# Hash attention and a gated block on Trainium2: the sign bits of two key chunks and two heads as four products on 32 rows each, side by side

## The chip, the cores and the metric

The kernel runs on one core of a Trainium2 chip. The core has TensorE (PE, matrix products), VectorE (DVE, elementwise work), ScalarE (ACT, activation functions and copies), GpSimd (POOL) and SyncE (SP). In this kernel POOL and SP mostly issue transfers (DMAs); ACT issues four at the start. Matmuls accumulate into PSUM, which has eight banks on each of its 128 partitions (rows); all else is held in SBUF, also of 128 partitions. The metric is the time of one execution on the device in microseconds. Each engine works through its own list of instructions in order, and waits on semaphores for what others have to deliver.

## The reference

There are 4 batches, 8 heads, 768 positions and a head width of 64. Each query and each key is projected on 6 directions, and the 6 signs make up its bucket. A query attends only to keys of its own bucket:

```
q_bits = einsum(q, proj) > 0            # 6 bits a query
k_bits = einsum(k, proj) > 0            # 6 bits a key
mask   = bucket(q_bits) == bucket(k_bits)
scores = where(mask, q @ k.T / sqrt(64), -1e9)
attn   = exp(scores - max) / sum
x      = (attn @ v), heads side by side # 3072 x 512
out    = (silu(x @ w_gate) * (x @ w_val)) @ w_out
```

The last line is the gated block, with 3072 tokens, 512 columns and 1536 hidden columns. The weights come in as doubles and are turned into fp32 parts on the chip, so that the products of the gated block can be made of several faster ones.

## The kernel before, in words

**Attention** goes through 16 pairs of heads (`pairs`: batch b, pair pr), two heads to a pair. The two heads of 64 dimensions lie above each other on the partitions: head 0 on rows 0 to 63, head 1 on rows 64 to 127, in the transposed tiles `qT` and `kT` (fp32, 128 x 768). A **unit** (`units`, line 503) is one pair n, one half of the queries (384) and one chunk c of 128 keys: 2 x 6 = 12 units a pair, 192 in all. Units 2i and 2i + 1 share pair and half, and their chunks are an even and the following odd one.

**A unit's scores** (`score`, line 533) are made in two steps. `products` (524) takes a two-bank PSUM buffer and puts into it keys times queries in fp32, head 0 into the one bank and head 1 into the other (`product`, 515, line 521). Each of these matmuls uses the 64 rows of its head, so that the two of them lie on different rows of the array. `mark` (528) then accumulates onto the same banks a bf16 product of sign bits: `kb` (bits of keys, times a large constant) with `qb` (bits of queries). It reaches its maximum only where all the signs agree, so after the exponential (L530, ACT) the weights of other buckets vanish. The exponential writes the weights `A` into a ring of 12 units.

**The bits.** One matmul with `hash_w` (`hash_blocks`, 427, L430) gives both heads' projections at once on a strip of 32 rows: rows 0 to 15 belong to head 0 and rows 16 to 31 to head 1. ACT takes the sign (L435) and puts it into rows 0 to 31 of `qb` or `kb` (`low`). The product of head h, however, reads rows h*64 to h*64 + 63, so the 32 rows must also stand at rows 64 to 95 (`high`). For queries a DMA on POOL's queue copies them (`spread_q`, L447). For keys two DVE instructions (`spread_k`, L444) write rows 64 to 95 and then rows 0 to 31, each multiplied with a column that keeps one head's 16 rows and zeroes the other's, and that brings in the large constant (`times_k`). The rest of the rows, 32 to 63 and 96 to 127, hold zeros from the start of the kernel, so that 64 rows can be multiplied. There are two tiles of each kind (`sides`), used in turn by even and odd pairs.

**Order.** The order is written out by hand (`manual_schedule`). For pair n the loop at line 632 transposes the raw tiles of pair n + 1 (`prepare_pair(2)`, DVE, L458), makes the 12 units' scores, adding up the weights on DVE between them (`add`, L563 to L570), then the sums over keys of pair n - 1 (`total`, L581), the projections of pair n + 1 (`hash_next` by way of `prepare_pair(1)`, L430) with the signs, and the spreads of the bits of pair n + 1. After that come pieces of weight preparation on ACT (`begin_pieces`) and DVE (`advance_pieces`), with their stores and loads on POOL's queue (L170, L130), and the twelve `attend` steps of pair n, which multiply the weights with the values (L545; here the two heads lie on 64 columns each). Pair 0 has a start of its own (`start_first`): its bits are spread by halves, and units 0 to 2 are made there.

**PSUM** is one pool of four buffers of two banks, taken in rotation: each unit's scores, the joint tile for sums and projections, the av tile, and later the tiles of the gated block.

**The gated block** follows when all pairs are done. It works on blocks of 1024 tokens, with matmuls on 128 rows and 128 columns (L690), and has no part in the change.

Of the kernel before, what the change touches and what calls it, by code (L numbers as in the profile page):

```python
# [13 lines left out]
ALU = mybir.AluOpType  # L14
# [5 lines left out]
def kernel(  # L20
# [20 lines left out]
    nc = tc.nc  # L41
    PSUM = bass.MemoryType.PSUM
    B, H, S, D = q.shape
    NBITS = proj.shape[1]
    P = 128
    NCH = S // P
    CH = NCH // 2
    HQ = CH * P
    BLOCK = 32
# [31 lines left out]
    def two_banks(name):  # L81
        return pp.tile([P, 2, 512], FP32, tag="pp", name=name)
# [21 lines left out]
    n = 0  # L104
# [197 lines left out]
    def attention(scope):  # L302
# [85 lines left out]
        mask, times_k = columns[2:4], columns[4:6]  # L388
# [3 lines left out]
        for h in range(2):  # L392
            rows = slice(h * D, (h + 1) * D)
# [18 lines left out]
        bits = {}  # L412
# [3 lines left out]
        def joint(n):  # L416

            if n not in joints:
                joints[n] = two_banks("joint")
            return joints[n]  # L420

        def front(n):
            bits["q", n] = sides["q", n % 2]
            bits["k", n] = sides["k", n % 2]
            low, high = slice(0, BLOCK), slice(D, D + BLOCK)

            def hash_blocks(todo):
                tile_ = joint(n - 2)[:, 1]
                for i, (name, half) in enumerate(todo):
                    nc.tensor.matmul(tile_[i * BLOCK : (i + 1) * BLOCK, 0:HQ], hash_w,  # L430
                                     T[name, n][:, half * HQ : (half + 1) * HQ],
                                     start=True, stop=True)

                def sign(i, name, half, to=low, **how):
                    nc.scalar.activation(bits[name, n][to, half * HQ : (half + 1) * HQ],  # L435
                                         tile_[i * BLOCK : (i + 1) * BLOCK, 0:HQ], AF.Sign,
                                         **(how or {"bias": nudge[name]}))

                return [lambda i=i, at=at, **how: sign(i, *at, **how) for i, at in enumerate(todo)]

            def spread_k(times, cols=slice(0, S)):
                b = bits["k", n][:, cols]
                for to, by in ((high, times[1]), (low, times[0])):
                    nc.vector.tensor_scalar(b[to], b[low], scalar1=by, scalar2=None, op0=ALU.mult)  # L444

            def spread_q():
                nc.gpsimd.dma_start(bits["q", n][high], bits["q", n][low])  # L447

            def hash_next(todo):
                q0, q1, *ks = hash_blocks(todo)  # L450
                q0()
                q1()
                spread_q()
                return ks + [lambda: spread_k(times_k)]

            def transpose_blocks(name):
                T[name, n] = opnd.tile([P, S], FP32, tag=name + "T", name=name + "T")
                nc.vector.transpose(T[name, n], raws[name, n].rearrange("p c h d -> p (c h d)"))  # L458

            def start_first():  # L460
                for half in range(2):
                    cols = slice(half * HQ, (half + 1) * HQ)
                    for name in "kq":
                        if not half:
                            T[name, n] = opnd.tile([P, S], FP32, tag=name + "T", name=name + "T")
                        ps = two_banks("tps")[:, 0]
                        for i in range(CH):
                            nc.tensor.transpose(ps[:, i * P : (i + 1) * P],
                                                raws[name, n][:, half * CH + i].rearrange("p h d -> p (h d)"),
                                                ident)  # L470
                        if name == "k":
                            nc.scalar.activation(T[name, n][:, cols], ps[:, 0:HQ], AF.Copy,
                                                 scale=2 / OFF)
                        else:
                            nc.vector.tensor_copy(T[name, n][:, cols], ps[:, 0:HQ])

                def both_heads(sign, name, half):
                    cols = slice(half * HQ, (half + 1) * HQ)
                    sign()
                    if name == "k":  # L480
                        spread_k(mask, cols)
                    else:
                        nc.vector.tensor_copy(bits["q", n][high, cols], bits["q", n][low, cols])

                products(0)
                todo = [("k", 0), ("q", 0), ("k", 1), ("q", 1)]
                signs = hash_blocks(todo)
                for i in range(2):
                    both_heads(signs[i], *todo[i])
                products(1)  # L490
                products(2)
                for i in range(3):
                    mark(i)
                    if i < 2:
                        both_heads(signs[2 + i], *todo[2 + i])

            order = [("q", 0), ("q", 1), ("k", 0), ("k", 1)]
            if n:
                return [lambda name=name: transpose_blocks(name) for name in "kq"] + [
                    lambda: hash_next(order)]  # L500
            return start_first()

        units = [(n, half, c) for n in range(len(pairs)) for half in range(2) for c in range(NCH)]
# [6 lines left out]
        def weights(u):  # L510
            return ring[u % RING]

        banks_of = {}

        def product(u, x, start):
            n, half, c = units[u]
            qs = slice(half * HQ, (half + 1) * HQ)
            ks = slice(c * P, (c + 1) * P)
            for h in range(2):
                rows = slice(h * D, (h + 1) * D)  # L520
                nc.tensor.matmul(banks_of[u][:, h], x["k", n][rows, ks], x["q", n][rows, qs],  # L521
                                 start=start, stop=not start)

        def products(u):
            banks_of[u] = two_banks("sc")[:, :, 0:HQ]
            product(u, T, True)

        def mark(u):
            product(u, bits, False)
            nc.scalar.activation(weights(u)[:, :, 0:HQ], banks_of.pop(u), AF.Exp,  # L530
                                 scale=SCALE * (1.0 if units[u][0] else OFF / 2))

        def score(u):
            products(u)
            mark(u)

        def attend(u):
            n, half, c = units[u]
# [81 lines left out]
        def prepare_pair(count):  # L620
            for _ in range(count):
                if steps:
                    rest.extend(f for f in steps.pop(0)() or [] if f)

        front(0)
        steps = front(1)
        last = []
        PACE = [2] * 4 + [1] * 4 + [2, 1] * 4
# [3 lines left out]
        for n in range(len(pairs)):  # L632
            u = 2 * NCH * n
            more = n + 1 < len(pairs)
            if n and more:
                steps = front(n + 1)
                prepare_pair(2)
            for i in range(2 * NCH):
                if u + i > 2:
                    score(u + i)  # L640
                if n == 0 and i == TURN:
                    prepare_pair(2)
                if i % NCH:
                    add(u + i)
                if i == (2 if n else TURN):
                    load(n + 2, "qk")
# [26 lines left out]
    with ExitStack() as scope:  # L673
        attention(scope)
# [258 lines left out]
```

## Time and profile before

| | |
|---|---|
| Time, median of 3 runs | 912.94 us (912.37 to 913.92) |
| The profiled execution's own time | 913.47 us |
| Its span in the profile | 911.4 us |
| PE busy | 904.0 us (99%) |
| DVE busy | 666.6 us (73%) |
| ACT busy | 448.0 us (49%) |
| POOL busy | 97.0 us (11%) |
| Granted PE clock | 0.999 |
| First and last score product starts at | 7.4 and 308.8 us |

How to read it: the profile is that of one execution. A group is one line's instructions of one kind, named by the tile that is written and the tiles that are read, with count, busy time, mean duration in ns, and what the engine had waited for before. PE stands for matmuls and PEld for the loads of their weights, which can overlap the matmuls. Shapes such as 64*128 are rows and columns of the array that a matmul uses; 64x384 is the operand that streams through. An fp32 matmul appears as two records. Matmuls are pipelined and their ends are modelled, so that the time from one start to the next is what one costs. In the timeline a line has start, duration, engine, line, operation, tiles, count, and in brackets the idle time ahead of it with its releaser. In the chain that ended last, each line has start, duration, and what filled it.

### The profile page before, as it was taken

What the parts mean: (1) busy time and instruction counts of PE and PEld (TensorE: products, weight loads), DVE (VectorE), ACT (ScalarE), POOL (GpSimd) and SP (SyncE); (2) the same over time, 40 slices, a digit from 0 to 9 for tenths busy, and PEclk for the clock granted to TensorE, in tenths of its full rate; (3) what the DMA queues carried; (4) which work ended last, traced back from release to release, by engine and by line L of the source; (5) the groups of instructions that cost most, each with busy time, mean ns of one, the idle gap of its engine ahead of it and who ended that gap; (6) DMA issues with size and microseconds to landing.
All of it is one profiled execution on the core that took longest, in us unless ns stands there. A gap on an engine that the chain in (4) does not pass through costs nothing.

```text
span 911.4 us, 12610 instructions
## 1 busy us (share of the span) xinstructions
PE 904.0 (99%) x4795; PEld 636.1 (70%) x4795; DVE 666.6 (73%) x774; ACT 448.0 (49%) x604; POOL 97.0 (11%) x193
## 2 busy tenths in 40 slices
PE   8999999999999999999999999999999999999998
PEld 4444444444444488888888888888888888888886
DVE  5889999989988968779785855465668754474746
ACT  6889888878888655452414243331313233413220
POOL 1111111011111120000100000101000100001000
PEclk9999999999999999999999999999999999999999
DMA  7777788787897599685756562444434642525332
GB/s 180 132 188 199 195 214 192 162 193 208 224 227 211 200 382 331 218 289 207 297 177 238 202 259 104 173 139 157 155 139 151 242 147 97 207 70 208 104 139 93
DMA packets 145579, 174.25 MB, mean 191 GB/s; under 512 B 106496, under 2 KB 115200, under 8 KB 145520
## 3 DMA queue, kind: packets, MB, share of 16 engines
q0 software_dynamic: 22864, 116.36, 36.4%
q1 hardware_dynamic: 121056, 56.71, 24.9%
q8 instruction: 38, 0.62, 0.3%
q10 hardware_dynamic: 1600, 0.39, 0.2%
q14 instruction: 21, 0.17, 0.1%
HBM read 133.17 MB, written 39.42 MB: 189 GB/s over the span
## 4 chain that ended last, share of the span: by engine, by line
PE 97%; DVE 1%; DMA 1%; ACTq 0%; issue 0%; ACT 0%; DVEq 0%
PE a L690 29%; PE o L690 22%; PE sc L521 17%; PE n L690 14%; PE av L545 13%; PE joint L581 1%; PE joint L430 1%; DMA vraw<-in_v_dram 1%; DMA kraw<-in_k_dram 0%; DVE both L567 0%; DVE both L563 0%; DVE acc L570 0%; ACTq L329 0%; DVE kb L444 0%; DVE kT L458 0%
## 5 line engine op out<-in xcount | busy, mean ns | idle before, releaser
L690 PE MATMUL a<-xparts,ring 128*128 128x512 f32 x1152 | 273.0, 389 | 0.0
L690 PEld LDWEIGHTS a<-xparts,ring 128*128 128x128 f32 x1152 | 216.1, 188 | 45.5 <-issue 0.6
L690 PE MATMUL o<-ring,hid 128*128 128x512 f32 (+1 forms) x870 | 199.1, 388 | 0.0
L690 PEld LDWEIGHTS o<-ring,hid 128*128 128x128 f32 x870 | 162.1, 188 | 35.2 <-DVE hid L745 1.0
L521 PE MATMUL sc<-qT,kT 64*128 64x384 f32 x768 | 156.9, 487 | 0.6 <-ACT A L530 0.6
L530 ACT ACTIVATE A<-sc 128x768 f32<-128x768 f32 x192 | 151.8, 815 | 7.5 <-PE sc L521 4.2
L690 PE MATMUL n<-xparts,ring 128*128 128x512 f32 x576 | 142.2, 389 | 0.0
L545 PE MATMUL av<-A,vraw 128*64 128x386 f32 (+1 forms) x768 | 127.7, 488 | 0.0
L690 PEld LDWEIGHTS n<-xparts,ring 128*128 128x128 f32 x576 | 108.1, 188 | 22.5
L735 DVE TENSOR_TENSOR v<-v,n 128x1024 f32<-128x1024 f32 x36 | 44.0, 1221 | 98.7 <-PE n L690 98.0
L248 POOL DMA_DIRECT2D ring<-ram x108 | 56.9, 529 | 499.9 <-PE n L690 328.4
L545 PEld LDWEIGHTS av<-A,vraw 128*64 128x64 f32 x768 | 53.7, 136 | 73.3 <-issue 63.4
L521 PEld LDWEIGHTS sc<-qT,kT 64*128 64x128 f32 x768 | 67.6, 187 | 48.5 <-issue 46.3
L729 ACT ACTIVATE g<-a 128x1024 f32<-128x1024 f32 x36 | 37.0, 1027 | 130.8 <-PE a L690 126.6
L740 ACT ACTIVATE hid<-v 128x1024 fp32r<-128x1024 f32 x36 | 38.2, 1062 | 114.5 <-DVE v L739 114.5
L737 ACT ACTIVATE g<-g 128x1024 f32<-128x1024 f32 x36 | 38.2, 1062 | 86.0 <-DVE g L735 86.0
L792 DVE TENSOR_TENSOR o<-o 128x512 f32<-128x512 f32 x92 | 63.0, 687 | 20.6 <-ACT o L786 18.2
L735 DVE TENSOR_TENSOR g<-g,n 128x1024 f32<-128x1024 f32 x36 | 43.8, 1217 | 32.7 <-PE n L690 32.7
L521 PE MATMUL sc<-qb,kb 64*128 64x384 bf16 x384 | 63.4, 323 | 1.1 <-DVE kb L444 1.1
L567 DVE TENSOR_TENSOR both<-both,A 128x1536 f32<-128x1536 f32 x32 | 56.2, 1757 | 3.2
L563 DVE SCALAR_TENSOR_TENSOR both<-A 128x1536 f32<-128x1536 f32 x32 | 55.7, 1741 | 3.5 <-ACT A L530 1.9
L743 DVE SCALAR_TENSOR_TENSOR hid<-hid,v 128x1024 fp32r<-128x1024 f32 x36 | 44.0, 1224 | 19.2 <-ACT hid L740 19.1
(79 smaller groups left out, 696.8 us busy)
## 6 DMA issues: line engine op xcount, KB each, us to landing
ring<-ram POOLq DMA_DIRECT2D x108, 768.0 KB, 5.1
ram<-stage POOLq DMA_DIRECT2D x23, 768.0 KB, 5.6
ram<-stage SPq DMA_DIRECT2D x13, 768.0 KB
qraw<-in_q_dram SPq DMA_DIRECT2D x64, 96.0 KB
vraw<-in_v_dram SPq DMA_DIRECT2D x16, 384.0 KB
out_dram<-o SPq DMA_DIRECT2D x23, 256.0 KB
kraw<-in_k_dram SPq DMA_DIRECT2D x60, 96.0 KB
r<-sums SPq DMA_DIRECT2D x30, 192.0 KB
```

The source lines that it names most:

```text
L248: nc.gpsimd.dma_start(t.bitcast(FP32), ram[at].bitcast(FP32))
L521: nc.tensor.matmul(banks_of[u][:, h], x["k", n][rows, ks], x["q", n][rows, qs], start=start, stop=not start)
L530: nc.scalar.activation(weights(u)[:, :, 0:HQ], banks_of.pop(u), AF.Exp, scale=SCALE * (1.0 if units[u][0] else OFF / 2))
L545: nc.tensor.matmul(ps[h * D : (h + 1) * D, 0:width], raws["v", n][:, h, c, :], a[:, h, 0:width], start=c == 0, stop=c == NCH - 1)
L563: nc.vector.scalar_tensor_tensor(out=t, in0=first, scalar=S * EPS / P / 2, in1=now, op0=ALU.add, op1=ALU.add)
L567: nc.vector.tensor_tensor(t, t, now, op=ALU.add)
L690: nc.tensor.matmul(ps, w, x, start=start, stop=stop)
L735: nc.vector.tensor_tensor(two(z), two(z), n_, op=ALU.subtract)
L737: nc.scalar.activation(z, z, AF.Silu)
L740: nc.scalar.activation(h, val, AF.Copy, scale=TOWARD / STEP)
L743: nc.vector.scalar_tensor_tensor(out=l, in0=h.bitcast(FP32), scalar=-STEP, in1=val, op0=ALU.mult, op1=ALU.add)
L792: nc.vector.tensor_tensor(accs[c], accs[c], t[:, 1], op=ALU.subtract)
```

## The change

Two consecutive units of a pair (one even and one odd key chunk) are now made together. `score` issues the fp32 products of both, and then four sign products, one for each head and each of the two chunks, each on 32 rows of its own: head h and chunk parity x use rows h*64 + x*32 to h*64 + x*32 + 31. The four write into four different banks. After them come the two exponentials. Pair 0 (the first 12 units) is left as it was.

For this the bits have to stand elsewhere. `spread_all` takes the place of `spread_k` for pairs 1 to 15: four DVE instructions of 384 columns each, in place of two of 768. Each writes one strip of 32 rows, and on it only the even or only the odd key chunks, in three blocks of 128 columns. `spread_q` copies the query bits to three strips (rows 32, 64 and 96) by three DMAs, where one copied them to row 64.

```diff
+            def spread_all(times):
+                b = bits["k", n].rearrange("p (c x q) -> p c x q", x=2, q=P)
+                for x in (1, 0):
+                    for h in (1, 0):
+                        to = slice(h * D + x * BLOCK, h * D + (x + 1) * BLOCK)
+                        nc.vector.tensor_scalar(b[to, :, x], b[low, :, x], scalar1=times[h],
+                                                scalar2=None, op0=ALU.mult)
+
             def spread_q():
-                nc.gpsimd.dma_start(bits["q", n][high], bits["q", n][low])
+                for to in range(BLOCK, P, BLOCK):
+                    nc.gpsimd.dma_start(bits["q", n][to : to + BLOCK], bits["q", n][low])
...
-                return ks + [lambda: spread_k(times_k)]
+                return ks + [lambda: spread_all(times_k)]
...
+        def exponential(u):
+            nc.scalar.activation(weights(u)[:, :, 0:HQ], banks_of.pop(u), AF.Exp,
+                                 scale=SCALE * (1.0 if units[u][0] else OFF / 2))
+
         def mark(u):
             product(u, bits, False)
-            nc.scalar.activation(weights(u)[:, :, 0:HQ], banks_of.pop(u), AF.Exp,
-                                 scale=SCALE * (1.0 if units[u][0] else OFF / 2))
+            exponential(u)
 
         def score(u):
-            products(u)
-            mark(u)
+            if u < 2 * NCH:
+                products(u)
+                mark(u)
+            elif u % 2 == 0:
+                products(u)
+                products(u + 1)
+                for h in range(2):
+                    for x in range(2):
+                        n, half, c = units[u + x]
+                        rows = slice(h * D + x * BLOCK, h * D + (x + 1) * BLOCK)
+                        nc.tensor.matmul(banks_of[u + x][:, h],
+                                         bits["k", n][rows, c * P : (c + 1) * P],
+                                         bits["q", n][rows, half * HQ : (half + 1) * HQ],
+                                         start=False, stop=True)
+                exponential(u)
+                exponential(u + 1)
```

## The prediction

> **What bounds the kernel now.** I read the page first (busy shares, the costliest groups), then the chain that ended last, in order of time, then the timeline of TensorE (PE) alone around one score stage, and last the rows of the operations that the change touches. From the page:
>
> ```profile
> PE 904.0 (99%) x4795; PEld 636.1 (70%) x4795; DVE 666.6 (73%) x774; ACT 448.0 (49%) x604; POOL 97.0 (11%) x193
> ...
> L521 PE MATMUL sc<-qT,kT 64*128 64x384 f32 x768 | 156.9, 487 | 0.6 <-ACT A L530 0.6
> L530 ACT ACTIVATE A<-sc 128x768 f32<-128x768 f32 x192 | 151.8, 815 | 7.5 <-PE sc L521 4.2
> ...
> L521 PE MATMUL sc<-qb,kb 64*128 64x384 bf16 x384 | 63.4, 323 | 1.1 <-DVE kb L444 1.1
> ```
>
> PE is busy throughout, and the score matmuls waited 1.7 us in all. The page says that ends of matmuls are modelled, so I count from start to start. One step of the chain repeats for nearly every pair of heads:
>
> ```profile
> 203.05 9.89 PE sc L521 x72
> 212.94 0.78 PE joint L581 x8
> 213.72 0.65 PE joint L430 x8
> 214.37 7.91 PE av L545 x48
> ```
>
> The chain has nothing but PE in it, 19.23 us a pair (183.82 to 203.05). The timeline of PE in that pair's scores, then at their end:
>
> ```profile
> 201.59 1.46 PE L545 MATMUL av<-A,vraw 128*64 128x384 f32 x8
> 202.98 0.92 PE L521 MATMUL sc<-qT,kT 64*128 64x384 f32 x4
> 203.73 0.33 PE L521 MATMUL sc<-qb,kb 64*128 64x384 bf16 x2
> 203.89 0.81 PE L521 MATMUL sc<-qT,kT 64*128 64x384 f32 x4
> 204.54 0.33 PE L521 MATMUL sc<-qb,kb 64*128 64x384 bf16 x2
> 204.70 0.81 PE L521 MATMUL sc<-qT,kT 64*128 64x384 f32 x4
> 205.34 0.33 PE L521 MATMUL sc<-qb,kb 64*128 64x384 bf16 x2
> ```
>
> ```profile
> 193.38 0.33 PE L521 MATMUL sc<-qb,kb 64*128 64x384 bf16 x2
> 193.64 0.85 PE L581 MATMUL joint<-acc,ones 128*32 128x384 f32 x8
> ```
>
> A unit takes 0.807 us (204.54 to 205.34). The sign products, both heads side by side, hold PE for 0.161 us (204.54 to 204.70), the fp32 products for 0.645: four slots of 0.161 and one more. A slot is S = 0.161.
>
> The second thing to see is the **price of a change of tile shape**. Two av groups start 0.325 apart; the last starts at 202.56, so its feed ends at 202.885, but the first score product starts at 202.98: a gap of 0.095. That first unit then needs 0.75 us for its fp32 part in place of 0.645: 0.105 more, because the first weights couldn't be loaded ahead. From scores to the joint matmuls (128*32) it is the same: 193.38 + 0.161 = 193.54, next start 193.64. From joint to av (194.65 + 0.325 = 194.975, next 195.07) it is 0.095. Where the tile shape stays (fp32 to bf16 scores, L581 to L430) there is no gap. Check: 12 x 0.807 + 24 x 0.325 + 1.30 (joint) + three changes (0.20 + 0.12 + 0.15) = 19.25, against 19.23 measured. So each change of shape is paid for in full on the bounding engine.
>
> How much of the first weight load shows depends on its kind. Mean LDWEIGHTS are 187 ns (128 columns fp32), 136 (64), 110 (32) and 94 (128 columns bf16): about 84 fixed, and 103, 52, 26 and 10 beyond it. Those excesses match what is exposed: 0.105 at the scores, about 0.05 at av (195.07 to the next load at 195.45 in place of 0.325), 0.02 at joint. For bf16 a unit whose weights came late shows it:
>
> ```profile
> 13.33 0.34 PE L521 MATMUL sc<-qb,kb 64*128 64x384 bf16 x2 [0.38 <-DVE kb L444]
> 13.50 0.57 PE L521 MATMUL sc<-qT,kT 64*128 64x384 f32 x2
> ```
>
> 0.17 in place of 0.161: exposed 0.01.
>
> **What the Trainium skill says.** "TensorEngine Tiling (Array Packing)", Key Properties: changing the tiling mode, not just the tile, drains TensorE; its list has 64*128 and 32*128 as different modes. The trace agrees for every change of shape that it has (0.095 to 0.10), a change of row height alone among them: from the 128*128 transposes (last start 7.20, spacing 0.11) to the 64*128 scores at 7.40, a gap of 0.09. No run here has 32 rows. "TensorE: Matmul & The Clock Gate", Measured speedup vs the span model: four row tiles of 32 rows ran 3.07 times as fast, each started about 4 ns after the one before. The trace shows only four column tiles, started within 0.02 us of each other (8.60 to 8.62), which agrees. The first page's Gotcha 1: different row tiles must not use one PSUM bank at once; here the four outputs lie in four banks (two buffers of two).
>
> **The change part by part.** It holds for 90 couples of units, six in each of 15 pairs; the first pair's 12 units stay.
>
> Removed: for each couple two slots of sign products become one: 0.161, so 6 x 0.161 = 0.97 us a pair.
>
> Added on PE, for each couple: into 32 rows, a gap of 0.095, an exposed bf16 load of 0.01, and three later starts in the group of four, 0.015: 0.12. Back to 64 rows: 0.095 + 0.10 for fp32 weights = 0.195. The last couple's way back is the change to joint, already paid today. A pair: 6 x 0.12 + 5 x 0.195 = 1.70. Neither is shown for 32 rows. Bounds: nothing, if row heights can be mixed freely (0 a pair); 0.20 each way, if the bf16 load is exposed as fp32's is (6 x 0.20 + 5 x 0.20 = 2.2). I take 1.70, since all changes in the trace have the gap.
>
> Net on PE: 1.70 - 0.97 = +0.73 a pair, 15 x 0.73 = +11.0 us.
>
> ScalarE (ACT): the exponentials of a couple now both come after its sign products, so the first starts about 0.65 + 0.1 later than today. Twelve take 9.73 us in the timeline (0.811 each), just as long as PE's twelve units. A couple on PE becomes 8 x 0.161 + 0.161 + 0.315 = 1.76, over ACT's 2 x 0.811 = 1.62, so ACT keeps up. Four PSUM buffers: a couple needs those of two couples before, whose exponentials end while PE is in the couple between. After the last sign products ACT is busy some 0.24 + 1.62 = 1.9 us, so the signs of the next pair (behind them on ACT) start about 0.3 later than now; they aren't needed for 8 us. Nothing, covered by the av stage's 7.9 us.
>
> VectorE (DVE): two L444 of 768 columns (2 x 408 ns) become four of 384. The row shows 307 as its minimum, which is that of the short form:
>
> ```profile
> L444 DVE TENSOR_SCALAR kb<-kb,columns x34: 307/408/414, 9.8 to 297.3; 32x768 bf16<-32x768 bf16 x30, 32x384 bf16<-32x384 bf16 x4
> ```
>
> 4 x 307 - 816 = +0.41 us a pair; bounds 0.2 (the columns alone, halved) and 1.6, if stepping over blocks of 128 halves the rate or worse. DVE is busy 14.4 to 18.5 us of 19.2 a pair, and the period grows by 0.73. The consumer, the first sign product, now comes 0.75 later in its stage. One pair is short today:
>
> ```profile
> 107.50 0.34 PE L521 MATMUL sc<-qb,kb 64*128 64x384 bf16 x2 [0.73 <-DVE kb L444]
> ```
>
> There PE waited 0.73 for the masked bits. The scores of the pair before began at 86.52; the bits were ready at 107.36, 20.84 later, and would be 21.25 after it. They'd be wanted at 19.33 + 0.73 + 1.39 + 0.10 = 21.55. So this wait goes: -0.7 us once.
>
> GpSimd (POOL): one q copy (0.52 us to issue, landing 2.1 to 5.3 us after) becomes three of 48 KB, 1.04 us later for the last and 1.4 MB more in 15 pairs. At the pair above the last would be issued at 100.6 and land by 105.9, wanted after 107.5. Behind them on POOL's queue come the piece stores (L170) and loads (L130), which sit waiting some 8 us a pair for exponentials. Nothing, so long as that wait exceeds 1 us. SP's queue gets nothing.
>
> Sum: the profiled execution took 913.47 us (span 911.4 and 2.1 around it). 913.47 + 11.0 - 0.7 = 923.8. The median shown, 912.94, is 0.5 below that execution, so **923.3 us**. The gated block, 593 us after the scores, only moves.
>
> **Rivals.**
> 1. Row heights mix without a drain (ends faster). For it: fp32 and bf16 scores at one shape follow without a gap. Against it: every change of shape has one. Then PE would need 1.45 us a couple, and ACT's 1.62 would bind: with exponentials from 1.8 us on, the second unit of couple six waits for the eighth exponential at 8.3, and the stage ends near 9.1 in place of 9.7. That is 0.3 (where DVE, at 18.5 + 0.4 us a pair, binds next) to 0.65 us a pair: 904 to 908. It decides below an average of 0.97 / 11 = 0.088 us a change, against my 0.15. Chance 0.10.
> 2. A lower price: no load is exposed, or the gaps are somewhat shorter. 11 x 0.095 + 6 x 0.015 - 0.97 = +0.17 a pair; with gaps of 0.07, -0.11: 911 to 915 with the 0.7 taken off. Chance 0.06.
> 3. The four don't run side by side (a wait between the tiles, or two at a time). The saving is gone: 15 x 0.97 = 14.5 more, 938, or half of that, 930. For: no four row tiles in this trace. Against: 64-row tiles do pair up, four column tiles do too. Chance 0.12.
> 4. The copies or the spread come late: the third q copy behind a 768 KB store, or DVE's four at the slow bound. A wait of 0.5 to 2 us in most pairs: 930 to 950. Against: over 7 us lie between issue and use. Chance 0.06.
>
> My case: 0.66, by itself 918 to 928.
>
> **How the numbers follow.** Left out below: rival 1 (0.10) and a sliver of rival 2. Left out above: half of rival 3 (0.06) and half of rival 4 (0.03). So 913 to 933 holds 0.8. About 0.2% (1.8 us) is what a measurement of this kernel can tell. Faster is rival 1, 0.10; the same is most of rival 2, 0.05; slower the rest, 0.85.
>
> **What would show it.** In the PE timeline after: four bf16 products of 32x384 starting within 0.02 us, a gap of about 0.1 before and after each group, the first fp32 products after it about 0.1 long over 0.645, a couple at 1.76 us and a pair at about 20. Rival 1 has no gaps, 1.62 a couple and PE waiting for L530; rival 3 shows starts 0.16 apart; rival 4 shows PE waiting for L444 or a DMA into qb. My sum is wrong if the gap depends on which shapes meet, or if ACT waits appear on PE.

## The result, and the profile after

The changed kernel takes 922.47 us (median; 922.35 to 922.5), against 912.74 us before (four executions; 912.94 was the median of the first three): a ratio of 1.0106, with a 95% interval of 1.009 to 1.0122. It is slower by 9.7 us. The prediction was 923.3 us, with 918 to 928 for its likeliest case.

The page of the kernel after. The new `score` begins at line 545: L530 makes the fp32 products (`product`), L556 the four sign products, L538 the exponential.

```profile
PE 914.1 (99%) x4795; PEld 625.6 (68%) x4795; DVE 675.4 (73%) x804; ACT 439.8 (48%) x604; POOL 112.1 (12%) x223
...
L538 ACT ACTIVATE A<-sc 128x768 f32<-128x768 f32 x192 | 145.0, 812 | 33.5 <-PE sc L556 32.6
L530 PE MATMUL sc<-qT,kT 64*128 64x384 f32 x768 | 150.4, 508 | 0.6 <-ACT A L538 0.6
```

TensorE is still 99% busy, with as many matmuls (4795) and no new wait. Its busy time grew by 10.1 us although the sign products now share the array: a time counted as busy is not all work. ACT now waits 32.6 us for the sign products, where it waited 4.2 for its scores: it isn't what holds the kernel.

The chain that ended last (start, duration, what filled it), for one pair:

```profile
207.91 1.49 PE sc L530 x8
...
218.49 0.78 PE joint L607 x8
219.27 0.65 PE joint L430 x8
219.92 7.91 PE av L571 x48
227.83 1.49 PE sc L530 x8
```

A pair takes 19.92 us (207.91 to 227.83) in place of 19.23. The parts outside the scores are as long as before (0.78, 0.65, 7.91), so the scores alone grew, by 0.69 a pair: 15 x 0.69 = 10.4. The gated block begins at 327.5 us in place of 318.5; that is 9.0 of the 9.2 us between the spans. The other 1.4 of the 10.4 were won elsewhere. Before, the three pairs around the wait for masked bits took 19.34, 20.13 and 19.31 us from one start of av to the next, 1.1 more than three times 19.23, and 0.73 of that is the wait itself; after, no pair is longer than the others. And the first score product of this execution starts 0.3 earlier (7.1 in place of 7.4).

The timeline of PE in these scores (start, duration, engine, line, tiles, count):

```profile
207.84 1.56 PE L530 MATMUL sc<-qT,kT 64*128 64x384 f32 x8
209.33 0.34 PE L556 MATMUL sc<-qb,kb 32*128 32x384 bf16 x4
209.60 1.56 PE L530 MATMUL sc<-qT,kT 64*128 64x384 f32 x8
211.09 0.34 PE L556 MATMUL sc<-qb,kb 32*128 32x384 bf16 x4
211.36 1.56 PE L530 MATMUL sc<-qT,kT 64*128 64x384 f32 x8
...
218.15 0.34 PE L556 MATMUL sc<-qb,kb 32*128 32x384 bf16 x4
218.42 0.85 PE L607 MATMUL joint<-acc,ones 128*32 128x384 f32 x8
```

Here is the whole loss. The four sign products really run side by side: they start within 0.01 us of each other, and from their start to the next fp32 product there are 0.27 us, one slot of 0.161 and 0.11 more. But eight slots of fp32 products are 1.29 us, and they take 1.49 (207.84 to 209.33), 0.20 more. The starts of the single matmuls in the trace divide this. From the first fp32 products of the couple to the second there are 0.425 us (207.835 to 208.260) in place of two slots, 0.322: 0.10 for the first weights, which weren't loaded ahead. From the last fp32 products to the signs there are 0.423 (208.905 to 209.328): 0.10 for the way into 32 rows. The 0.11 after the signs is the way back and the bf16 weights; the trace doesn't separate them, but by the figures of before they would be 0.10 and 0.01. A couple takes 1.764 (209.600 to 211.364). Without any change of shape it would be 9 x 0.161 = 1.45, and before it was 1.61.

### The profile page after: what moved, and what is told of

Same layout as the page of the kernel before. It is cut to its first block, busy times and chain, and to the rows that moved or that the text cites. A ratio compares the mean times of both kernels' runs of the same rounds, so it can differ in the third digit from the quotient of the medians.

```text
span 920.6 us, 12707 instructions
## 1 busy us (share of the span) xinstructions
PE 914.1 (99%) x4795; PEld 625.6 (68%) x4795; DVE 675.4 (73%) x804; ACT 439.8 (48%) x604; POOL 112.1 (12%) x223
## 4 chain that ended last, share of the span: by engine, by line
PE 99%; DMA 0%; ACTq 0%; ACT 0%; DVE 0%; issue 0%; DVEq 0%
PE a L716 28%; PE o L716 21%; PE sc L530 16%; PE n L716 14%; PE av L571 14%; PE sc L556 3%; PE joint L607 1%; PE joint L430 1%; DMA kraw<-in_k_dram 0%; ACTq L329 0%; PE tps L477 0%; ACT A L538 0%; DVE kb L444 0%; ACT kb L435 0%; DVE o L842 0%
## 5 line engine op out<-in xcount | busy, mean ns | idle before, releaser
L538 ACT ACTIVATE A<-sc 128x768 f32<-128x768 f32 x192 | 145.0, 812 | 33.5 <-PE sc L556 32.6
L530 PE MATMUL sc<-qT,kT 64*128 64x384 f32 x768 | 150.4, 508 | 0.6 <-ACT A L538 0.6
L530 PEld LDWEIGHTS sc<-qT,kT 64*128 64x128 f32 x768 | 66.1, 186 | 48.8 <-issue 13.0
L814 DVE SCALAR_TENSOR_TENSOR o<-o 128x512 f32<-128x512 f32 x71 | 48.7, 686 | 10.8 <-PE o L716 10.6
```

The costliest lines, as they stand in the source:

```text
L814: nc.vector.scalar_tensor_tensor(out=accs[c], in0=t[:, 0], scalar=STEP + 1, in1=accs[c], op0=ALU.mult, op1=ALU.add)
```

## The experiments

Theory: each change of tile shape costs about 0.1 us of gap plus the load that can't be hidden, and this outweighs the merged slot. Rival A: the later exponentials make the loss. Rival B: the extra copies and spreads do. Rival C: four tiles of 32 rows are slow. The first five runs tell these apart. Their edits are shown against the changed kernel unless the text says otherwise, and shortened; a line in plain words stands for the code that it describes. Each ratio is to the kernel before, measured beside that run.

**The couple order alone.**

```diff
-                for h in range(2):          # four products on 32 rows
-                    ...
+                product(u, bits, False)     # 64 rows, as before
+                product(u + 1, bits, False)
                 exponential(u)
                 exponential(u + 1)
...                                          # spread_q and spread_k as before
```

> The couple order alone: fp32 products of both units, then their four sign products on 64 rows as before, then both exponentials; bits and copies as before. My theory (each change of tile shape costs about 0.11 us into 32 rows and 0.20 back, the merged group saves 0.16): nothing is left of either, so the time of before, 912.0 to 913, perhaps less the 0.7 us wait for the masked bits. Rival A (the later exponentials make the loss): 918 to 923.

Measured: 912.18 us, ratio to before 0.9994 (0.9985 to 1.0002). Its chain, two successive pairs:

```profile
201.78 9.89 PE sc L529 x72
...
221.01 9.89 PE sc L529 x72
```

19.23 us, the pair of before. Rival A falls: the order costs nothing. Four bf16 products between fp32 ones don't cost anything either, so long as all have 64 rows: it is the shape, not the type. The wait of 0.73 us for the masked bits doesn't appear in its profile.

**The same shapes, unit by unit.** This doubles the changes of shape and merges nothing.

```diff
-                products(u)
-                products(u + 1)
-                for h in range(2):
-                    for x in range(2):
+                products(u)
+                for h in range(2):          # two products, strip c % 2
...
-                exponential(u)
-                exponential(u + 1)
+                exponential(u)
```

> The new bits, but unit by unit: two sign products on 32 rows after each unit's fp32 products, so nothing is merged and each pair has 12 ways into 32 rows and 11 back. My theory: 12 x 0.105 + 11 x 0.195 = 3.4 us a pair, 15 pairs: 912.7 + 51 - 0.7 = 963 (958 to 968). Rival A (order of the exponentials): about 913, since that order is back to what it was. Rival B (the extra copies and spreads): 922, as the change.

Measured: 963.85 us, ratio 1.0559 (1.0543 to 1.0575), 51.2 us above before. The timeline of PE at the end of a pair, and the chain from one pair to the next:

```profile
199.60 0.92 PE L530 MATMUL sc<-qT,kT 64*128 64x384 f32 x4
200.45 0.33 PE L554 MATMUL sc<-qb,kb 32*128 32x384 bf16 x2
200.71 0.85 PE L604 MATMUL joint<-acc,ones 128*32 128x384 f32 x8
```

```profile
300.89 0.84 PE sc L530 x4
...
323.58 0.85 PE sc L530 x4
```

The fp32 products hold PE for 0.85 (199.60 to 200.45) in place of 0.645, the sign products 0.26 (200.45 to 200.71) in place of 0.161; a unit takes 1.11 and a pair 22.69. That is 3.46 more than before, for 12 ways in and 11 back: 0.15 each, as the sum of the prediction had it (3.4). Rivals A and B had this run at 913 and 922.

**The side work alone.** This edit is against the kernel before.

```diff
+                for to in range(BLOCK, P, BLOCK):      # three query copies
+                    nc.gpsimd.dma_start(bits["q", n][to : to + BLOCK], bits["q", n][low])
...
+                for to, by in ((high, times[1]), (low, times[0])):
+                    for x in (1, 0):                    # four spreads of 384 columns
+                        nc.vector.tensor_scalar(b[to, :, x], b[low, :, x], scalar1=by, ...)
```

> The side work alone: the kernel before, with four spread instructions of 384 columns in place of two of 768, and three query copies in place of one; the products are those of before. My theory: hidden but for the one pair in which the masked bits are late today, where 0.55 us more on VectorE shows: 912.7 to 913.5. Rival B (the side work makes the loss): 918 to 923.

Measured: 913.27 us, ratio 1.0005 (0.9997 to 1.0014). Rival B falls as the cause of 10 us; up to about 1.3 us (the end of the interval) can't be excluded.

**One shape, no change.**

```diff
-                products(u)
-                products(u + 1)
+                four(T, start=True, stop=False)    # fp32 on the unit's own strip
+                four(T, start=False, stop=False)   # and once more
+                four(bits, start=False, stop=True)
```

> One shape for all score products: each unit's fp32 products run on the 32-row strip of its sign products too, four side by side, twice. Each unit thereby multiplies only the 32 dimensions of its own strip, and those twice; the other 32 are left out. The matmul time is that of the change, without a change of shape inside the scores. My theory: nine slots of 0.161 a couple without gaps, 1.45 us, so ScalarE at 1.62 a couple becomes the bound: 903 to 909, with TensorE waiting for the exponentials. Rival C (four tiles of 32 rows are slow by themselves): 920 or more.

Measured: 915.41 us (913.21 to 918.06), ratio 1.0026 (1.0019 to 1.0034). The gaps are gone and with them 7 us of the loss, but the time isn't below 909. What TensorE waited for, the group of its weight loads shows:

```profile
L558 PEld LDWEIGHTS sc<-qT,kT 32*128 32x128 f32 x1440 | 86.8, 184 | 46.9 <-ACT A L538 18.8
```

Loads waited for exponentials. Two readings of this were open: 32-row tiles are slow, or the two units in lockstep need two free PSUM buffers at once. So a second form let the odd unit run half a unit behind:

```diff
+                strips of u, first half of its fp32 work
+                signs(u - 1); exponential(u - 1)
+                strips of u, second half, beside u + 1, first half
+                signs(u); exponential(u)
+                strips of u + 1, second half
...                                          # add() one unit later
```

> One shape for all score products again, with each unit's fp32 products on its own strip, twice (the other 32 dimensions are left out), but the odd unit runs half a unit behind the even one, so that a strip doesn't have to wait for two PSUM buffers at the same time; the additions on VectorE come one unit later. My theory: the shortfall of the run with one shape came from the lockstep of the two units over four PSUM buffers (its weight loads waited for L538), not from 32 rows: 6 x 9 + 4 = 58 slots of 0.161, 9.35 us for the scores of a pair and 18.9 to 19.1 a pair, as VectorE allows, 906 to 912. Rival (32-row tiles are slow by themselves, or ScalarE at 0.81 an exponential binds): 915 or more.

Measured: 914.92 us (913.45 to 917.26), ratio 1.0024 (1.0017 to 1.0031). The time missed the theory's 906 to 912, but the timeline of PE settles the question of the tiles:

```profile
204.30 0.36 PE L554 MATMUL sc<-qb,kb 32*128 32x384 bf16 x2
204.37 0.93 PE L554 MATMUL sc<-qT,kT 32*128 32x384 f32 x8
205.02 0.33 PE L554 MATMUL sc<-qb,kb 32*128 32x384 bf16 x2
205.11 0.88 PE L554 MATMUL sc<-qT,kT 32*128 32x384 f32 x8
205.75 0.36 PE L554 MATMUL sc<-qb,kb 32*128 32x384 bf16 x2
```

A couple takes 1.45 us (204.30 to 205.75): nine slots, no gap. 32-row tiles run at full pace, and rival C falls. The lockstep run has such couples too, before exponentials hold it up (283.13 to 284.58, from one group of signs to the next). That its calm pairs still took 19.17 us is then put down to the buffers; no run tested them alone. The starts of av lie 18.75 us apart in the calm pairs (136.03 to 154.78). The gain is given back elsewhere; PE's waits in this profile (`kb` are the masked bits, `ring` the gated block's weights):

```profile
PE sc L554 <- DVE kb L451: 2.6, 4, 0.6
PE joint L430 <- DVE qT L467: 1.5, 3, 0.9
...
PE a L736 <- DMA ring<-ram: 1.2, 1, 1.2
```

With PE faster, VectorE's bits and transposes are late in some pairs, and the gated block waits for its weights. Eight of the fifteen pairs are longer than the calm ones, by about 7 us together. So the gated block begins at 317.3 us, no earlier than in the couple order alone (317.2). The merge itself has a gain, about 0.48 us a pair in the calm pairs of this form, and what takes it away in the change is the shape; but nothing of the gain arrived at the end. This form isn't a kernel for use, since half the dimensions are missing; the true fp32 products would need both halves of a head on each strip.

**Half the changes of shape.**

```diff
+                flip = u // 2 % 2       # every second couple: signs first
                 four sign products with start=bool(flip), stop=not flip
+                if flip: product(v, T, False) for both units
```

> Half the changes of shape: every second couple has its four sign products first, right after those of the couple before, and its fp32 products after them; all else is as in the change. If the number of changes alone decides: 3 x 0.12 + 3 x 0.195 - 0.97 = -0.02 us a pair, 911.5 to 912.7. My theory adds a second limit, PSUM: the early sign products need the buffers of the couple before last, whose exponentials end only at about 5.2 and 8.8 us of the stage, so TensorE waits some 0.3 and 0.45 us for L538 in each pair, and the stage ends near 10.5 in place of 9.8: 920 to 924.

Measured: 914.3 us (913.11 to 916.74), ratio 1.0021 (1.0012 to 1.003). The chain:

```profile
203.60 1.49 PE sc L530 x8
205.09 0.44 PE sc L560 x8
205.53 2.78 PE sc L530 x16
...
222.82 1.49 PE sc L530 x8
```

A pair takes 19.22 us, as the count of changes says (19.21), and no wait for PSUM shows: that part of my theory was wrong. The eight sign products of two couples stand together, with one gap before and one after (0.44 for two slots). So with six changes a pair the merging just pays for them. In the profile the loss is elsewhere: four pairs take 19.65, 19.96, 19.91 and 19.41 us from av to av, about 2 us more than four calm ones, and PE waits there for the masked bits:

```profile
PE sc L560 <- DVE kb L451: 1.3, 2, 0.6
```

**Only where the way out is paid anyway.**

```diff
+                if u % (2 * NCH) < 2 * NCH - 2:
+                    product(u, bits, False)
+                    product(u + 1, bits, False)
+                else:
                     four sign products on 32 rows
...
+                # the last key chunk's bits on the second strip too: two spreads of 128 columns
```

> The four on 32 rows only for the last couple of each pair, where the change of shape on the way out (to the joint matmuls) is paid for anyway; the other five couples as in the run with the couple order alone. The bits of the last key chunk stand on both strips of a head, so that unit 5 gets its sign sum doubled. My theory: 0.12 - 0.16 = -0.04 us a pair: 19.19 us a pair in place of 19.23, 911.3 to 912.1, 0.6 below the couple order alone. Rival (merging never pays, whatever stands beside it): 0.3 us or more above the couple order alone.

Measured: 913.66 us (912.63 to 916.05), ratio 1.0017 (1.0009 to 1.0025). The timeline of PE at the end of a pair, then the chain of two pairs:

```profile
209.64 1.46 PE L538 MATMUL sc<-qT,kT 64*128 64x384 f32 x8
211.03 0.34 PE L568 MATMUL sc<-qb,kb 32*128 32x384 bf16 x4
211.30 0.85 PE L619 MATMUL joint<-acc,ones 128*32 128x384 f32 x8
```

```profile
182.35 9.57 PE sc L538 x68
...
201.53 9.57 PE sc L538 x68
```

19.18 us a pair: merging pays by 0.05 there, as worked out (0.04). Yet the kernel as a whole was 1.4 us above before, not 0.5 below. In its profile the gated block began at 316.9, 0.3 before that of the couple order alone, and PE then waited 0.9 us for `ring<-ram`. I suspected the extra copies on POOL's queue, and ran two more kernels. The first is this one with an edit:

```diff
-                    nc.gpsimd.dma_start(...)                       # strips 32 and 96 on SP
+                    (nc.gpsimd if to == D else nc.sync).dma_start(...)
```

> As the run with only the last couple on 32 rows, but the two extra query copies go out on SP's queue, so that POOL's queue holds just the transfers it held before. My theory now: that run's stages were shorter (19.18 us a pair) and its time was lost at POOL, whose third ring load at the start of the gated block went out 2.06 us after the second: so 911.3 to 912.0 here, and no such pause. Rival (the merged couple itself costs, or VectorE's two extra spreads do): 913 to 914.5 again.

Measured: 919.43 to 923.35 us in four executions, ratio 1.0096 (1.0081 to 1.0111); the expectation was missed by 8 us and more. A fifth execution, the one that was profiled, took 4812.57 us with TensorE at a fifth to a sixth of its pace throughout. No other execution showed this, its cause isn't known, and nothing is concluded from it. The same kernel again, for a profile at its usual pace:

> The same kernel as the run with the two extra query copies on SP's queue, whose profile showed TensorE at about a sixth of its pace from start to end and can't be read. My theory for its other times (919 to 923): the copies stand on SP's queue behind some 9 us of raw loads and ahead of the row of sums, so that VectorE waits longer for that row in each pair (0.5 us and more, against 3 us in all in the change), and the masked bits come late: 919 to 923 again, with waits of PE for VectorE's bits or of VectorE for the row. Rival (the slow pace of TensorE is the kernel's own): it shows again in most executions.

Measured: 920.08 us, ratio 1.0085 (1.0058 to 1.0113). In its profile PE waits five times, 4.7 us together, for a query copy (DMA `qb<-qb`). The chain at one of these waits:

```profile
99.71 2.75 SPq L337
105.68 2.79 DMA qb<-qb
108.51 6.99 PE sc L539 x50
```

The time is in the expected range, but not by the expected waits. The query copies themselves were late: they went out on SP only at 105.68 us, behind the raw loads (L337), while the copy on POOL had gone out at 99.97; and the products on 64 rows read those strips too. VectorE's wait for the row of sums (14.1 us), which I had expected to grow, explains little: it was 12.7 in the kernel before. So SP is the wrong place for these copies. The other run has the couple order alone, with three copies on POOL; its edit is against the couple order alone:

```diff
-                nc.gpsimd.dma_start(bits["q", n][high], bits["q", n][low])
+                for to in range(BLOCK, P, BLOCK):
+                    nc.gpsimd.dma_start(bits["q", n][to : to + BLOCK], bits["q", n][low])
```

> The couple order alone (all sign products on 64 rows, two spreads), with three query copies on POOL's queue in place of one. My theory: the pause of about 2 us between POOL's ring loads shows again, and 0.5 to 1.5 us more than the couple order alone, 912.7 to 913.7. Rival (the extra copies cost nothing): 912.0 to 912.4.

Measured: 912.48 us, ratio 0.9997 (0.9989 to 1.0005). POOL's timeline at the start of the gated block:

```profile
322.89 1.21 POOL L248 DMA_DIRECT2D ring<-ram  x2 [2.05 <-issue]
```

The pause of 2 us is there, and costs nothing. It could not have been the cause in the last-couple run either: the load that PE waited for there landed at 328.79 us, and had been issued before the pause. POOL's timeline of that run:

```profile
315.90 0.56 POOL L170 DMA_DIRECT2D ram<-stage  x1 [10.72 <-DVE stage L168]
...
319.36 0.53 POOL L248 DMA_DIRECT2D ring<-ram  x1
```

This load stands on POOL's queue behind stores that wait for VectorE's piece of weight preparation (`stage`, L168). In the couple order alone the same store goes out at 315.27 and the load at 318.75, both 0.6 earlier, though PE reaches the gated block 0.3 later there. So it was VectorE, by way of POOL's queue, that was behind.

The traces say the same of the pairs. In the couple order alone VectorE has finished the masked bits 0.6 to 5.3 us before the first sign product of a pair, and in the change 1.15 to 4.8. In the runs with shorter scores they are finished only as that product starts (0.15 us ahead) in some pairs: three with half the changes, four with one shape, five with the staggered units, two with the last couple. The kernel before has two such pairs as well. That VectorE's extra spreads (0.55 us a pair, 0.49 with the last couple alone) bring this about fits, since three copies without them leave 0.8 us or more, but no run took the spreads out of a shorter form, so it was not shown. The larger spread of these runs' times (913.21 to 918.06 with one shape) stays open: a profile shows one execution.

No version tried is clearly faster than the kernel before. The couple order alone is the lowest of them, and its interval includes no change.

## Why the prediction was right

- **The changes of shape** (0.12 a way in and 0.195 a way back, together 0.315): held. The trace has 0.31 for both (0.20 in the stretch of the fp32 products, 0.11 in that of the signs), and a couple of 1.764 against 1.76. The run unit by unit, with 23 changes a pair, gives 0.15 a change, the average that I had taken. So rivals 1 and 2, with no gaps or a lower price, are out.
- **The merged slot** (0.97 a pair): held. Four products take one slot (0.27 less the gap and load), and their starts lie within 0.01 us; with the shape kept, a couple takes nine slots. So rival 3 is out.
- **The net** (+0.73 a pair, +11.0): measured +0.69 and 10.4. From the couple order alone (912.18) to the change (922.47) there are 10.3 us.
- **The wait for masked bits** (-0.7 once): it is gone, as argued. The size can't be told more closely: the couple order alone, which lacks this wait too, lies 0.47 us below before by the medians (912.18 and 912.65), with an interval from 1.4 below to 0.2 above.
- **ScalarE "keeps up" at 0.811 an exponential**: the conclusion was right, the figure wrong. ACT's timeline after:

```profile
209.76 1.51 ACT L538 ACTIVATE A<-sc 128x768 f32<-128x768 f32 x2 [0.95 <-PE sc L556]
211.54 1.51 ACT L538 ACTIVATE A<-sc 128x768 f32<-128x768 f32 x2 [0.26 <-PE sc L556]
```

Two exponentials of 812 ns fill 1.51 us, so the second starts 0.70 after the first: they overlap. The 0.811 that I read from twelve in 9.73 us was TensorE's pace, not ScalarE's; the trace of before already had two exponentials 0.75 apart (206.58 and 207.33). So rival 1's price (904 to 908, "ACT's 1.62 would bind") was argued wrongly: at two times 0.70, an estimate from these starts, ACT allows 1.40 a couple, and the run with the staggered units found VectorE and the ring's weights in the way. It did not touch the forecast, where PE needs 1.76.

- **VectorE's spreads** (+0.41 a pair, bounds 0.2 and 1.6): mis-sized, and hidden in the change. The row of the new spreads:

```profile
L451 DVE TENSOR_SCALAR kb<-kb,columns x60: 337/342/346, 26.1 to 303.9; 32x384 bf16<-32x384 bf16 x60
```

4 x 342 in place of 816: +0.55, since three blocks of 128 columns took 35 ns more than the plain 384 (307). It stayed hidden because each pair became 0.69 longer.
- **POOL's copies** (nothing): held. 15 x 3 copies of 515 ns; no wait of PE for `qb` or for the spreads' `kb` from pair 1 on in the change. So rival 4 is out.

## What to carry to other kernels

Count the changes of tile shape before merging small products into another shape. Here a visit to the other shape and back took 0.31 us out of the engine that bounds (two gaps of about 0.10, 0.10 for the first fp32 weights, about 0.01 for the bf16 ones), and one merged slot of 384 columns returned 0.161. Two slots for one visit just broke even (19.22 us a pair against 19.23), and where the way out was paid for anyway the pair was 0.05 shorter. Neither made the kernel faster: in the traced executions VectorE was next in line. So before counting a gain on the engine that bounds, see how far ahead of it the other engines are. And read an engine's pace from start to start while it isn't waiting: a row of instructions without idle time may just be following another engine.

## What the runs showed of the hardware that I had not expected

- Exponentials of 128x768 overlap: they are 812 ns long and start 0.69 to 0.71 us apart when their inputs are ready (four in a row from 224.68 us with half the changes, two by two in the change).
- fp32 products on four tiles of 32 rows keep the pace that two tiles of 64 have, 0.161 us a slot: 1.45 us for nine slots, with fp32 on two tiles beside bf16 on the others as well.
- A visit of two products to 32 rows costs almost as much as one of four: 0.26 us to the next fp32 product in the run unit by unit, and 0.27 in the change.
